# The sign of float64 weight words as an exponent bit, conversions queued behind a rectifier, and more unread products at a norm

## The chip, the cores and the metric

The kernel runs on one NeuronCore of a Trainium2 chip, in one launch. The metric is the device time of one execution in microseconds (us). TensorE does the matrix products, VectorE and ScalarE the elementwise work, GpSimd (POOL in the rows) some of it, and SyncE (SP) issues the transfers.

## The reference

A linear attention over 32 learned memories, then a Fourier mixing of tokens and features, a norm and a feed-forward layer with a residual. Eight batches of 576 tokens, 8 heads of 64 features, so 512 features; all float32.

```python
a = softmax(phi, over seq)                       # (b, h, s, 32)
k_m, v_m = a^T k, a^T v                          # (b, h, 32, 64)
x = softmax(q k_m^T / 8) v_m                     # heads joined: (8, 576, 512)
u = x + real(fft(fft(x, axis=1), axis=2))
un = (u - mean(u)) / sqrt(var(u) + 1e-6)
out = u + relu(un @ w_ch1) @ w_ch2               # w_ch1 512 x 2048, w_ch2 2048 x 512
```

The two weight matrices arrive as float64 words and are read as pairs of 32-bit words; the kernel itself makes float32 of them.

## The kernel before, in words

The 4608 tokens are 36 tiles of 128, taken two at a time as 18 *chunks*. The hidden width of 2048 is cut into 8 *units* (`NW`) of 256: unit j holds 1 MB of `w_ch1` and 1 MB of `w_ch2` as float64. A generator (`background`) makes the tiles of `u` batch by batch; the main loop advances it between units.

**Start.** Batch 0's attention is computed in float32, then its mixing, then `norm_chunk(0)` (called after `keep_busy(KEEP[4])`): bn_stats per tile (L777), a power on GpSimd (L787), the normalised tile `un` (L788), eight transposes on TensorE into `pt_unT` (L803), and copies on ScalarE (L804). `keep_busy(n)` (L262 to 266) issues 2n products of `identf` with itself into a PSUM tile `idle` that nothing reads.

**Chunk 0, the direct stage.** Chunk 0's feed-forward runs in float32 straight from the converted weights, unit by unit: `prepare_w1(j)` converts unit j of `w_ch1`, `ffn1_direct(j)` makes the hidden values (L821, two halves `ph`, 8 float32 products in the rows for each) and rectifies them on ScalarE (L824), `stage_w2(j)` converts unit j of `w_ch2`, `ffn2_direct(j)` accumulates the output `po` (L838, 8 in the rows for a unit). Beside it batch 1's scores run (`psc`, L576 to L613), and each unit is split into a float16 high and low part for the later chunks (`split_w1`, L953 to L958).

**The conversion** is `to_f32` (L907 on). `hi` is the upper 32-bit word of a float64 (sign, 11 exponent bits, 20 mantissa bits), `lo` the lower one. ScalarE reads `hi` as a float32 and writes its absolute value times 2^-112 (L919), which brings the exponent into 8 bits' room; VectorE shifts the word left by 3 (L921), ors in the sign bit taken from `hi` (L922), and ors in the top 3 bits of `lo` (L932). Then ScalarE squares the result and sums it (L943) for a scale; a one-column product `as_sq` (L239) adds over the partitions. Unit 0 of each matrix is converted in two halves (`HALVED`).

**Order.** All is written with a tile framework that sorts each engine's instructions by its own estimate. `issue_after(x)` makes instructions stand behind x in x's own engine queue; `after(names, ...)` does so for marked instructions, and the tables `GATE1` and `GATE2` name those that unit j's conversions stand behind. Each engine works its queue strictly in order.

**Later chunks** (1 to 17) use three float16 products for each float32 one: `ffn1` (L288, tile `ph`) and `ffn2` (L874).

Of the kernel before, what the change touches and what calls it, by code (L numbers as in the profile page):

```python
# [10 lines left out]
F32 = mybir.dt.float32  # L11
# [4 lines left out]
AF = mybir.ActivationFunctionType  # L16
ALU = mybir.AluOpType
# [22 lines left out]
NHS = 7  # L40
STEPS = 2
NX = 2
KEEP = [8, 18, 0, 0, 10, 4, 3]
GATE1 = [["et0"]] + [["un1", "uh0"]] * 7
GATE2 = [["at0"]] + [["un1", "uh0"]] * 7
NA = 2
# [87 lines left out]
def kernel(  # L134
# [10 lines left out]
    nc = tc.nc  # L145
# [116 lines left out]
    def keep_busy(n):  # L262

        with tc.issue_after(marks["pe"].ins) if "pe" in marks else nullcontext():
            for _ in range(2 * n):
                nc.tensor.matmul(idle, lhsT=unread[:, :P], rhs=unread, start=True, stop=True)
# [51 lines left out]
    def pooling_f32(b, pl, pf, rest):  # L318
# [11 lines left out]
        if b == 0:  # L330
            keep_busy(KEEP[1])
        for g in range(2):
# [7 lines left out]
        for g in range(2):  # L340
# [5 lines left out]
            if b == 0:  # L346
                keep_busy(KEEP[5 + g])
            marks[f"et{b}"] = nc.vector.tensor_copy(out=et32[:, g, :4], in_=pt.rearrange("p (t c) -> p t c", c=P))
# [270 lines left out]
    def pair_transpose(b, g, ahl, attnT):  # L619
        transpose(attnT[:, g], ahl.rearrange("p t c -> p (t c)"), b == 0, f"attnT_{b}_{g}")  # L620

    def values(b, vmf, ivs, ahl):
# [4 lines left out]
        if b < NX:  # L627
# [3 lines left out]
            if b == 0:  # L631
                marks["pe"] = marks["sum"]
                for g in range(3):
                    pair_transpose(b, g, ahl.pop(g), attnT)
                keep_busy(KEEP[2])
            norm_scale(sg, isg, top, 1, 14, f"v_{b}")
# [177 lines left out]
    def ffn1_direct(j):  # L814

        w = w1_f32(j).rearrange("p (k c) -> p k c", k=NK)
        h = h_f32(j)
        for f in range(UB):
            ph = ps1.tile([P, CH, P], F32, tag="h", name=f"ph_0_{j}_{f}", padded_shape=[P, 4, P])
            for k in range(NK):  # L820
                nc.tensor.matmul(  # L821
                    ph, lhsT=w[:, k, f * P : (f + 1) * P], rhs=unTs[0][:, k], start=(k == 0), stop=(k == NK - 1)
                )
            nc.scalar.activation(h[:, f], ph, AF.Relu)  # L824

    def h_slot(c, j):
        return hring[:, (4 + c * NW + j) % NW]
# [82 lines left out]
    def to_f32(stages, dst, key):  # L910

        if key in HALVED:
            stages = [s[:, i * UW : (i + 1) * UW] for s in stages for i in range(2)]
        n = UW // len(stages)
        for i, stage in enumerate(stages):
            wf = stage.rearrange("p (a b) -> p a b", b=2)
            hi, lo = wf[:, :, 1], wf[:, :, 0]
            part = dst[:, n * i : n * (i + 1)]
            nc.scalar.activation(part, hi.bitcast(F32), AF.Abs, scale=2.0**-112)  # L919
            d = part.bitcast(I32)  # L920
            nc.vector.tensor_scalar(out=d, in0=d, scalar1=3, scalar2=None, op0=ALU.logical_shift_left)  # L921
            marks[key] = nc.vector.scalar_tensor_tensor(  # L922
                out=d, in0=hi, scalar=-0x80000000, in1=d, op0=ALU.bitwise_and, op1=ALU.bitwise_or
            )
            lu = lo.bitcast(U32)
            if key in LP:
                marks[key] = nc.vector.tensor_scalar(
                    out=lu, in0=lu, scalar1=29, scalar2=None, op0=ALU.logical_shift_right
                )
                nc.gpsimd.tensor_tensor(out=d, in0=lo, in1=d, op=ALU.add)  # L930
            else:
                marks[key] = nc.vector.scalar_tensor_tensor(  # L932
                    out=part.bitcast(U32),
                    in0=lu,
                    scalar=29,
                    in1=part.bitcast(U32),
                    op0=ALU.logical_shift_right,
                    op1=ALU.bitwise_or,
                )
        sq = tiny("sq", 2, 4)  # L940
        dump = elt.rearrange("p l c -> p (l c)").bitcast(BF16)[:, :UW]
        with soon(int(key[2:])):
            marks["sq" + key] = nc.scalar.activation(dump, dst, AF.Square, accum_out=sq[:, 0:1])  # L943
            return all_sum(sq[:, 0:1], 1, f"sq_{key}")
# [55 lines left out]
    marks = {}  # L1000
# [77 lines left out]
    for g in range(NG):  # L1078
        with tc.issue_after(marks["q"].ins):
            marks["q"] = nc.sync.dma_start(  # L1080
                out=phi_next[:, :, g], in_=raw[1, g, :, KV:KVP].rearrange("p (t c) -> p t c", t=NST)
            )
    keep_busy(KEEP[0])
    first = [load_pair(0, 0)]
# [40 lines left out]
    def after(names, fn, *a):  # L1125
        with ExitStack() as st:
            for m in names:
                st.enter_context(tc.issue_after(marks[m].ins))
            return fn(*a)
# [17 lines left out]
    while made < 2:  # L1147
        made, room = next(bg)
    keep_busy(KEEP[4])
    unTs = {0: norm_chunk(0)}  # L1150
    hs = {c: [] for c in range(n_chunks)}
    po = [ps2.tile([P, 512], F32, tag="o", name=f"po_0_{t}") for t in range(CH)]
    for j in range(NW):
        if j > 2:
            load_weights(j)
        after(GATE1[j], prepare_w1, j)
        ffn1_direct(j)
        after(GATE2[j], stage_w2, j)
        ffn2_direct(j, po)
        with soon(j):  # L1160
            split_w1(j)
        advance(0, steps=STEPS)
        if made >= 2 * CH and 1 not in unTs:
            unTs[1] = norm_chunk(1)
# [20 lines left out]
    for n in range(NW, n_steps):  # L1185
        c, j = divmod(n, NW)
# [75 lines left out]
```

## Time and profile before

| | |
|---|---|
| Median of 3 runs | 950.43 us (950.41 to 950.98) |
| Profiled execution, its own time | 948.53 us |
| Its span | 946.8 us |
| TensorE busy | 930.0 us (98%), 7784 products |
| VectorE busy | 560.6 us (59%), 1291 instructions |
| ScalarE busy | 458.8 us (48%) |
| GpSimd busy | 219.2 us (23%) |

The span is what the profiler sees from the first to the last instruction; the execution's own time is 1.7 us longer, and the median 1.9 us above that. Busy shares are means over the whole kernel: the start, the direct stage and the later chunks have different limits, so the rows below are read stretch by stretch. A granted clock of 1.00 is TensorE's 2.4 GHz, 0.50 its 1.2 GHz.

### The profile page before, as it was taken

The page shows a single profiled execution, that of the slowest core. Times are in us where ns is not written, and L with a number is a line of the kernel's source. Part 1 is how long each engine was busy: PE and PEld are TensorE (multiplying, and loading weights), DVE is VectorE, ACT ScalarE, POOL GpSimd, SP SyncE. Part 2 cuts the span into 40 slices and gives each one's busy share as a digit, 9 for nine tenths or more (in the row PEclk, how much of TensorE's full clock was granted, in tenths as well). Part 3 has the DMA queues.
Part 4 walks back from the last instruction along what each step waited for, and adds up shares of the span by engine and source line. Part 5 has one row for each costly group of instructions (what it writes and reads, how often), then busy time and mean ns, then how long its engine had stood idle before and what let it go on. Part 6 is the DMA issues. An engine that isn't in the chain of part 4 may idle for free.

```text
span 946.8 us, 18932 instructions
## 1 busy us (share of the span) xinstructions
PE 930.0 (98%) x7784; PEld 662.8 (70%) x7784; DVE 560.6 (59%) x1291; ACT 458.8 (48%) x920; POOL 219.2 (23%) x255
## 2 busy tenths in 40 slices
PE   9989899999999999999999999999999999999998
PEld 8966568677777777777767777777776667666664
DVE  5989987767665666666424666667656675221111
ACT  4666757856465545654414554756446544211110
POOL 1302533414132222423200241223121331200000
PEclk9999899999999999999999999999999999999999
DMA  9947540454126242644102641263133201110000
GB/s 316 388 179 266 168 117 1 83 136 102 43 49 172 60 86 42 153 101 93 23 24 59 139 102 43 56 153 103 31 69 73 82 19 48 28 45 22 2 23 23
DMA packets 115959, 88.09 MB, mean 93 GB/s; under 512 B 100384, under 2 KB 100384, under 8 KB 113824
## 3 DMA queue, kind: packets, MB, share of 16 engines
q1 hardware_dynamic: 115872, 86.87, 34.5%
q8 instruction: 61, 1.00, 0.5%
q14 instruction: 26, 0.21, 0.1%
HBM read 58.15 MB, written 9.44 MB: 71 GB/s over the span
## 4 chain that ended last, share of the span: by engine, by line
PE 82%; DVE 7%; ACT 2%; issue 1%; POOL 1%; DMA 0%; DVEq 0%
PE ph L288 36%; PE po L874 36%; PE pm L288 2%; PE pp_t L288 2%; PE px_t L288 1%; PE psc L288 1%; PE pa L684 1%; DVE w2s L922 1%; DVE w1t L932 1%; DVE w2s L932 1%; PE pv L657 1%; PE pp_t L727 1%; DVE w1t L958 1%; DVE w1t L922 1%; PE pf L362 0%
## 5 line engine op out<-in xcount | busy, mean ns | idle before, releaser
L288 PE MATMUL ph<-unring,w1t 128*128 128x256 f16 x3264 | 389.0, 273 | 0.0
L874 PE MATMUL po<-w2s,hring 128*128 128x512 f16 x1632 | 378.8, 379 | 0.0
L288 PEld LDWEIGHTS <-w1t 128*128 128x128 f16 x3264 | 314.8, 98 | 64.0 <-issue 3.3
L874 PEld LDWEIGHTS <-hring 128*128 128x128 f16 x1632 | 157.1, 98 | 157.8 <-issue 0.4
L865 DVE SCALAR_TENSOR_TENSOR hring<-ph,hring 128x512 f16<-128x512 f32 x136 | 93.0, 684 | 155.2 <-ACT hring L864 155.1
L864 ACT ACTIVATE hring<-ph 128x512 f16<-128x512 f32 x136 | 80.3, 590 | 166.7 <-PE ph L288 163.8
L592 POOL TENSOR_TENSOR aring<-aring,scratch 128x384 f32<-128x384 f32 x28 | 24.2, 864 | 177.9 <-DVE scratch L590 169.0
L787 POOL TENSOR_TENSOR scratch<-scratch,small 128x1 f32<-128x1 f32 x36 | 22.6, 632 | 170.3 <-DVE scratch L786 118.5
L288 PEld LDWEIGHTS <-stg 128*128 128x128 f16 x1152 | 45.1, 98 | 8.5 <-issue 0.5
L808 POOL TENSOR_TENSOR ud<-un,ud 128x1024 f16<-128x1024 f32 x17 | 36.2, 2128 | 28.6 <-ACT ud L807 28.6
L586 ACT ACTIVATE aring<-aring,scratch 128x384 f32<-128x384 f32 x24 | 14.7, 611 | 54.6 <-DVE aring L585 54.6
L509 POOL TENSOR_TENSOR stg<-rawt,stg 128x640 f16<-128x640 f32 x12 | 17.4, 1454 | 87.3 <-ACT rawt L508 87.3
L838 PE MATMUL po<-w2s,hring 128*128 128x512 f32 x64 | 33.6, 657 | 3.4 <-DVE w2s L932 3.3
L611 ACT CAST aeo<-eo 128x384 f16<-128x384 f32 x30 | 15.3, 510 | 44.0 <-DVE eo L608 44.0
L886 DVE SCALAR_TENSOR_TENSOR uring<-po,small,uring 128x512 f32<-128x512 f32 x34 | 24.4, 742 | 16.9 <-PE po L874 16.9
L763 DVE SCALAR_TENSOR_TENSOR uring<-px_t,scratch,share 128x256 f32<-128x256 f32 (+1 forms) x80 | 34.1, 476 | 0.1
L749 DVE SCALAR_TENSOR_TENSOR share<-pp_t,scratch,small 128x257 f32<-128x257 f32 (+1 forms) x48 | 21.1, 481 | 21.1 <-ACT small L746 21.1
L602 POOL TENSOR_TENSOR aring<-aring 128x128 f32<-128x128 f32 x56 | 33.0, 609 | 2.0
L576 DVE TENSOR_REDUCE scratch<-psc 128x12 f32<-128x384 f32 x32 | 17.6, 551 | 26.4 <-PE pm L288 14.0
L288 PE MATMUL pm<-et,stg 128*128 128x64 f16 (+1 forms) x740 | 32.3, 195 | 0.3 <-DMA et<-elt 0.3
L613 DVE SCALAR_TENSOR_TENSOR aeo<-aeo,small,eo 128x128 f16<-128x128 f16 x30 | 24.1, 803 | 12.0 <-ACT aeo L611 12.0
L821 PE MATMUL ph<-unring,w1t 128*128 128x256 f32 x128 | 30.4, 384 | 0.7 <-DVE w1t L932 0.7
(271 smaller groups left out, 1227.8 us busy)
## 6 DMA issues: line engine op xcount, KB each, us to landing
out<-uring SPq DMA_DIRECT2D x36, 256.0 KB, 2.4
rawt<-in_raw SPq DMA_DIRECT2D x13, 640.0 KB, 4.6
stg<-in_raw SPq DMA_DIRECT2D x13, 640.0 KB, 5.1
stg<-in_w SPq DMA_DIRECT2D x7, 1024.0 KB, 5.0
rawt<-in_raw SPq DMA_DIRECT2D x15, 384.0 KB, 3.3
stg<-in_raw SPq DMA_DIRECT2D x15, 384.0 KB, 3.2
phs<-in_raw SPq DMA_DIRECT2D x28, 160.0 KB, 3.4
w2s<-in_w SPq DMA_DIRECT2D x4, 1024.0 KB, 10.2
```

The lines of the kernel that those rows point to most:

```text
L288: m = nc.tensor.matmul(out, lhsT=lhsT, rhs=rhs, start=start, stop=stop)
L592: eng.tensor_tensor(out=a, in0=a, in1=sm.unsqueeze(2).to_broadcast([P, 12, M]), op=ALU.mult)
L602: eng.tensor_tensor(out=a2[:, i : i + 4], in0=a[:, 0:4], in1=a[:, 4:8], op=op)
L613: marks[f"s{b}_{g}"] = nc.vector.scalar_tensor_tensor(out=lo[:, :4], in0=hi[:, :4], scalar=mk[:, 64:65], in1=eov[:, :4], op0=ALU.mult, op1 ...
L763: nc.vector.scalar_tensor_tensor(out=u[rows, hs], in0=px[rows, hs], scalar=igx[rows], in1=tm[rows, w * NJ + half : w * NJ + half + 256], o ...
L808: marks[f"ul{c}"] = nc.gpsimd.tensor_tensor(out=ud[:, 1], in0=un, in1=ud[:, 0], op=ALU.subtract)
L821: nc.tensor.matmul(ph, lhsT=w[:, k, f * P : (f + 1) * P], rhs=unTs[0][:, k], start=(k == 0), stop=(k == NK - 1))
L838: nc.tensor.matmul(po[t], lhsT=h[:, f, t], rhs=w[:, f], start=(j == 0 and f == 0), stop=(j == NW - 1 and f == UB - 1),)
L864: nc.scalar.activation(h[:, 0], phv, AF.Relu)
L865: nc.vector.scalar_tensor_tensor(out=h[:, 1], in0=phv, scalar=0.0, in1=h[:, 0], op0=ALU.max, op1=ALU.subtract)
L874: nc.tensor.matmul(po[t], lhsT=hs[j][:, lh, f * 2 + t], rhs=w2s[:, j * UB + f, lw, :], start=(j == 0 and f == 0 and i == 0), stop=(j == NW ...
L886: nc.vector.scalar_tensor_tensor(out=u, in0=po[t], scalar=cout if c else 0.5, in1=u, op0=ALU.mult, op1=ALU.add)
```

## The change

Three edits. (1) ScalarE's absolute value becomes its parametric rectifier (Prelu): out = x for x above 0, alpha times x below, with alpha = -2^32, behind the same scale. A negative weight comes out positive with its exponent 32 higher, which is bit 28 of the word; the shift by 3 moves bit 28 into the sign's place. The instruction that or-ed the sign in (L922 before) is gone: 20 of them. (2) The second rectifier of unit j's hidden values is marked `h{j}`, and from unit 2 on the conversions of unit j stand behind `h{j-2}` in ScalarE's queue. (3) `KEEP[4]` goes from 10 to 28: 56 unread products in place of 20 ahead of chunk 0's transposes.

```diff
-KEEP = [8, 18, 0, 0, 10, 4, 3]
+KEEP = [8, 18, 0, 0, 28, 4, 3]
...
-            nc.scalar.activation(h[:, f], ph, AF.Relu)
+            marks[f"h{j}"] = nc.scalar.activation(h[:, f], ph, AF.Relu)
...
-            nc.scalar.activation(part, hi.bitcast(F32), AF.Abs, scale=2.0**-112)
+
+            nc.scalar.activation(part, hi.bitcast(F32), AF.Prelu, scale=2.0**-112, alpha=-(2.0**32))
             d = part.bitcast(I32)
             nc.vector.tensor_scalar(out=d, in0=d, scalar1=3, scalar2=None, op0=ALU.logical_shift_left)
-            marks[key] = nc.vector.scalar_tensor_tensor(
-                out=d, in0=hi, scalar=-0x80000000, in1=d, op0=ALU.bitwise_and, op1=ALU.bitwise_or
-            )
...
-        after(GATE1[j], prepare_w1, j)
+        after(GATE1[j] + ([f"h{j - 2}"] if j >= 2 else []), prepare_w1, j)
         ffn1_direct(j)
-        after(GATE2[j], stage_w2, j)
+        after(GATE2[j] + ([f"h{j - 2}"] if j >= 2 else []), stage_w2, j)
```

In the changed kernel the conversion on ScalarE is L920, the shift L922, the or of the low bits L930, the square L941, the split's first part L951. The framework sorts the queues anew, so the order moves in many places; three matter.

VectorE just ahead of chunk 0's norm, where `w2s` is unit 0 of `w_ch2` in two halves, `share` and `uring` the mixing of the first two tiles; before the change:

```order
L921 TENSOR_SCALAR w2s<-w2s 128x512 x2
L922 SCALAR_TENSOR_TENSOR w2s<-w2s 128x512 x2
L932 SCALAR_TENSOR_TENSOR w2s<-w2s 128x512
L749 SCALAR_TENSOR_TENSOR share<-pp_t_617,scratch,small 128x257 x2
L932 SCALAR_TENSOR_TENSOR w2s<-w2s 128x512
L763 SCALAR_TENSOR_TENSOR uring<-px_t_633,scratch,share 128x256 x2
L763 SCALAR_TENSOR_TENSOR uring<-px_t_644,scratch,share 128x256 x2
```

The same place of VectorE's queue in the changed kernel:

```order
L922 TENSOR_SCALAR w2s<-w2s 128x512 x2
L930 SCALAR_TENSOR_TENSOR w2s<-w2s 128x512 x2
L749 SCALAR_TENSOR_TENSOR share<-pp_t_617,scratch,small 128x257 x2
L763 SCALAR_TENSOR_TENSOR uring<-px_t_633,scratch,share 128x256 x2
L763 SCALAR_TENSOR_TENSOR uring<-px_t_644,scratch,share 128x256 x2
```

The two sign instructions are gone and both low-bit instructions now stand ahead of the mixing.

ScalarE from the copies of chunk 0's transposed tile (L804) to unit 0's rectifiers (L824), before the change:

```order
L804 COPY unring<-pt_unT_691 128x4x128
L919 ACTIVATE w1t<-w1t 128x1024
L919 ACTIVATE w2s<-w2s 128x1024
L919 ACTIVATE w1t<-stg 128x1024
L919 ACTIVATE w2s<-stg 128x1024
L953 ACTIVATE w1t<-w1t,small 128x1024
L746 ACTIVATE small<-pp_t_745,scratch 128x255
L824 ACTIVATE hring<-ph_0_0_713 128x256
L943 ACTIVATE elt,scratch<-w1t 128x1024
L824 ACTIVATE hring<-ph_0_1_719 128x256
```

The same stretch of ScalarE's queue in the changed kernel:

```order
L804 COPY unring<-pt_unT_727 128x4x128
L920 ACTIVATE w1t<-w1t 128x1024
L920 ACTIVATE w2s<-w2s 128x1024
L951 ACTIVATE w1t<-w1t,small 128x1024
L746 ACTIVATE small<-pp_t_777,scratch 128x255
L941 ACTIVATE elt,scratch<-w1t 128x1024
L824 ACTIVATE hring<-ph_0_0_747 128x256
L824 ACTIVATE hring<-ph_0_1_753 128x256
L920 ACTIVATE w1t<-stg 128x1024
L920 ACTIVATE w2s<-stg 128x1024
```

The two conversions out of `stg`, those of unit 2, stood ahead of unit 0's rectifiers and now stand behind the second of them.

ScalarE in the middle of the direct stage, from unit 3's second rectifier to unit 4's second, in the changed kernel (`ahring`, `aeo`, `aring` belong to batch 1's scores):

```order
L824 ACTIVATE hring<-ph_3_1_975 128x256
L920 ACTIVATE w1t<-stg 128x1024
L920 ACTIVATE w2s<-hring 128x512
L920 ACTIVATE w2s<-uring 128x512
L611 CAST aeo<-eo 128x12x32
L586 ACTIVATE aring<-aring 128x384
L824 ACTIVATE hring<-ph_4_0_1035 128x256
L941 ACTIVATE elt,scratch<-w1t 128x1024
L941 ACTIVATE elt,scratch<-w2s 128x1024
L951 ACTIVATE w1t<-w1t,small 128x1024
L824 ACTIVATE hring<-ph_4_1_1041 128x256
```

Unit 5's conversions stand right behind unit 3's rectifier, and their squares stand ahead of unit 4's second one.

## Rows read from the trace of the kernel before

**Rows 1.** Busy time by stretch: us, then busy (instructions) of each engine, clock, DMA.

```profile
core 0: us, PE busy (x) PEld busy (x) DVE busy (x) ACT busy (x) POOL busy (x), PEclk, DMA share, GB/s
20.00:30.00 10.00, 10.00 (x92) 10.00 (x91) 9.97 (x28) 4.67 (x12) 1.56 (x2) 1.00 1.03 415
...
57.80:128.00 70.20, 64.58 (x277) 42.66 (x274) 70.03 (x131) 50.60 (x86) 20.04 (x18) 0.95 0.56 187
128.00:940.00 812.00, 811.67 (x7028) 572.46 (x7029) 446.83 (x1034) 377.97 (x766) 184.64 (x206) 1.00 0.29 69
```

**Rows 2.** TensorE in order of time around the norm: start, length, engine, line, names, count.

```profile
44.86 1.48 PE L288 MATMUL pp_t<-vh,at 128*128 128x257 f16 x12
...
47.07 2.35 PE L266 MATMUL idle<-identf 128*128 128x256 f16 x20
53.69 1.94 PE L803 MATMUL pt_unT<-identf,un 128*128 128x128 f32 x8 [4.27 <-DVE un L788]
...
55.52 1.91 PE L288 MATMUL pp_t<-vh,at 128*128 128x257 f16 x12
...
57.83 3.67 PE L821 MATMUL ph<-unring,w1t 128*128 128x256 f32 x16
```

**Rows 3.** Busy time by stretch, columns as in rows 1, around the transposes.

```profile
53.00:54.00 1.00, 0.31 (x2) 0.34 (x3) 0.93 (x2) 0.00 (x0) 0.58 (x1) 0.52 0.06 26
...
56.00:57.00 1.00, 1.00 (x9) 0.81 (x8) 0.31 (x4) 1.00 (x2) 0.00 (x0) 0.78 0.07 16
```

**Rows 4.** VectorE in order of time ahead of the norm.

```profile
45.95 1.30 DVE L922 SCALAR_TENSOR_TENSOR w2s<-w2s 128x512 int32<-128x512 int32 x2
47.15 0.70 DVE L932 SCALAR_TENSOR_TENSOR w2s<-w2s 128x512 uint32<-128x512 uint32 x1
...
53.00 1.16 DVE L788 TENSOR_SCALAR un<-uring,scratch 128x512 f32<-128x512 f32 x2 [0.60 <-POOL scratch L787]
```

**Rows 5.** TensorE in order of time in the direct stage.

```profile
77.77 1.96 PE L838 MATMUL po<-w2s,hring 128*128 128x512 f32 x4
...
81.40 1.45 PE L288 MATMUL psc<-scratch,rawt 128*128 128x64 f32 x12
...
94.78 3.69 PE L821 MATMUL ph<-unring,w1t 128*128 128x256 f32 x16
101.80 8.31 PE L838 MATMUL po<-w2s,hring 128*128 128x512 f32 x12 [3.32 <-DVE w2s L932]
...
121.97 1.13 PE L821 MATMUL ph<-unring,w1t 128*128 128x256 f32 x4 [0.72 <-DVE w1t L932]
...
127.99 0.40 PE L657 MATMUL pv<-hring,share 64*32 64x512 f16 x4 [1.45 <-ACT share L644]
```

**Rows 6.** VectorE by line, 57.8 to 128 us: busy, mean ns, idle before.

```profile
L958 DVE SCALAR_TENSOR_TENSOR w1t<-w1t,small 128x1024 f16<-128x1024 f32 x4 | 6.8, 1710 | 0.0
...
L921 DVE TENSOR_SCALAR w1t<-w1t 128x1024 int32<-128x1024 int32 (+1 forms) x8 | 5.2, 651 | 1.0 <-ACT w1t L919 1.0
L922 DVE SCALAR_TENSOR_TENSOR w1t<-stg,w1t 128x1024 int32<-128x1024 int32 x4 | 4.9, 1213 | 0.0
...
L922 DVE SCALAR_TENSOR_TENSOR w2s<-hring,w2s 128x512 int32<-128x512 int32 x1 | 2.6, 2611 | 0.0
...
L932 DVE SCALAR_TENSOR_TENSOR w1t<-w1t 128x1024 uint32<-128x1024 uint32 x2 | 2.4, 1204 | 0.0
```

**Rows 7.** ScalarE by line, 57.8 to 128 us.

```profile
L943 ACT ACTIVATE elt<-w1t 128x1024 bf16<-128x1024 f32 x7 | 7.4, 1056 | 1.9 <-DVE w1t L932 1.7 <-DVE small L260 0.2
...
L953 ACT ACTIVATE w1t<-w1t,small 128x1024 f16<-128x1024 f32 x6 | 6.9, 1145 | 1.4 <-DVE w1t L958 1.4
L824 ACT ACTIVATE hring<-ph 128x256 f32<-128x256 f32 x15 | 5.7, 380 | 2.7 <-PE as_sq L239 1.8 <-PE ph L821 0.9
L919 ACT ACTIVATE w1t<-stg 128x1024 f32<-128x1024 f32 x4 | 4.6, 1158 | 1.6 <-DMA stg<-in_w 1.6
```

**Rows 8.** ScalarE's only table load, in order of time.

```profile
0.73 1.28 ACT L185 ACT_TABLE_LOAD   x1 [0.73 <-PEq L1250]
```

## The prediction

> **What bounds the kernel now.** Read the stretches first. From 128 to 940 us TensorE is busy for 811.67 of 812.00 us at a granted clock of 1.00 [rows 1]: nothing that frees VectorE or ScalarE there can show. The direct stage, 57.8 to 128 us, is another matter: there VectorE is busy 70.03 of 70.20 us, TensorE 64.58, ScalarE 50.60, and the clock is 0.95 [rows 1]. VectorE is the full engine, and TensorE is what pays. TensorE's own list in order of time then shows where. Up to 98 us its products stand back to back; after that come three holes, 3.32 us, 0.72 us and 1.45 us long, the first two ended by VectorE's last conversion step and the third by a ScalarE copy [rows 5]. Behind the first hole 12 products of `po` take 8.31 us, where 4 of them took 1.96 us at 77.77 us [rows 5]; three times 1.96 is 5.9, so 2.4 us more go there to a lower clock. The stage thus loses 3.32 + 0.72 + 1.45 + 2.4 = 7.9 us of TensorE, and could not be shorter than 70.2 - 7.9 = 62.3 us.
>
> A second loss lies just ahead, at chunk 0's norm. TensorE issues its 20 unread products at 47.07 us, then stands idle for 4.27 us until VectorE has written `un` [rows 2]. The granted clock is 0.52 in the microsecond in which it starts again and has come back in part, to 0.78, by 56 to 57 us [rows 3]. So the transposes and the mixing product behind them run slowly: 12 `pp_t` products take 1.91 us at 55.52 and took 1.48 us at 44.86 [rows 2].
>
> **The change part by part.** *The sign off VectorE.* Twenty L922 instructions go: two halves of unit 0 of each matrix ahead of the norm, and the fourteen conversions of units 1 to 7 in the direct stage (two of these in halves). In the stage one of 1024 words takes 1.21 us [rows 6], 1.13 from start to start, so 14 x 1.13 = 15.8 us; one half took 2.61 us, 1.9 above its like [rows 6], and goes too. VectorE's work there falls from 70.0 to 52.3 us, under TensorE's 62.3. TensorE's three holes and the slow stretch behind the first then have no cause left in VectorE's throughput, and up to 7.9 us come back. ScalarE's 50.6 us stay as they are if Prelu costs what the absolute value did.
>
> *Prelu's price.* The trace has no Prelu. Three other functions over 1024 words cost 1.06 (square), 1.15 (scaled copy) and 1.16 us (absolute value) [rows 7]; I take 1.16, the row with the same operands. If it made two passes it would be 2.3 us: 14 x 1.16 = 16.2 us more on ScalarE, 66.8 in all, 4.5 above TensorE's floor. A gain is bounded by the square: 14 x 0.1 = 1.4 us off an engine that isn't full, so nothing.
>
> *The conversions behind the rectifiers.* No instruction is added; ScalarE's order changes. Unit j+2's two conversions now follow the second rectifier of unit j, and unit j is two units ahead of their use, so a conversion has about one unit of TensorE's time to get through ScalarE and VectorE: 62.3 / 8 = 7.8 us on average, against 1.16 for the conversion, 0.65 for the shift and 1.2 for the or [rows 6, 7], 3.0 us in all for the first matrix and about 5 for the second. What is queued behind the conversions is the next thing to be late. By the changed order a turn of ScalarE from one unit's second rectifier to the next one's holds two conversions (2.3), two squares (2.1), a split (1.15) and two rectifiers (0.76) [rows 7], and some 1.4 us of the scores' steps: 7.7 us of its own. The squares wait for VectorE, which I put at 1.5 us a turn. That makes 9.2 us in the units with scores, where TensorE needs 3.69 + 2 x 1.96 + 1.45 [rows 5], less some 0.6 of overlap, so 8.5; without scores 7.7 against 7.1. Over six turns ScalarE falls behind by 4 x 0.7 + 2 x 0.6 = 4.0 us, and TensorE gives 3.6 us of grace, since a second half's rectified values are read only after one half of `po` and the next `ph`. Little is left, some 0.4 us; to it I add about 2 us for single instructions that stretch, as the 2.61 did. So 2.5 us of new waits, with 0 and 6 as ends: 7.9 - 2.5 = **5.4 us gained** in the stage.
>
> *Norm and unread products.* Ahead of the norm VectorE loses two sign instructions at 45.95 us, 1.2 us from start to start, directly on its queue to `un` [rows 4]. Two more go at about 20 us, where VectorE is busy 9.97 of 10 us [rows 1]; how much of those 1.2 us arrives is unknown, between all and nothing. `un` is then ready 1.2 to 2.4 us sooner, which would start the transposes at 52.5 to 51.3. But 56 products at 2.35 / 20 us each [rows 2] take 6.6 us: begun at 47.07, or up to 1.2 us earlier, they end at 53.7 to 52.5. The products become the last wait, by a little. I take a start 0.8 us earlier, ends 0 and 1.2. With no hole ahead of them the transposes run at the full clock: 8 in 1.94 us at half clock [rows 2, 3], so about half of that saved, and 0.43 on the mixing product, 1.4 together; I take 1.3, and as ends 0.5 (a hole remains) and 1.8. Sum: **2.1 us gained**, 0.5 to 3.0.
>
> *Afterwards.* Chunks 1 to 17 need the splits of both matrices, made by ScalarE, VectorE and GpSimd while TensorE runs the first of them. All of this moves forward with the stage, and the changed order places `w_ch2`'s first splits only after two of chunk 1's hidden units rather than six. The 0.33 us of idle time there [rows 1] can grow; I take 0.3 more, ends 0 and 1.5.
>
> Sum: 2.1 + 5.4 - 0.3 = 7.2 us. The profiled execution's own 948.53 becomes 941.3; the median stands 1.9 above it, so **943.2 us**.
>
> **Rivals.** *ScalarE's queue takes VectorE's place (slower).* If nearly all of VectorE's work in a turn lies between a conversion and the second square, a turn is 1.16 + 6.9 + 1.06 + 1.15 + 0.38 = 10.7 us, with 6.9 from two shifts and two ors (3.7), a split (1.2) and the scores' reads (some 2). The loss is then 6 x (10.7 - 8.0) - 3.6 = 12.6 us in place of 7.9, and with the norm's 2.1 the time is 953.0. The point is a turn of about 10.6 us, where the loss reaches 7.9 + 2.1 + 1.9. With a split at the mean of 1.71 [rows 6] and one stretched row a turn it is 13 us and the time near 965. For it: the squares do stand ahead of the next rectifier, and rows of VectorE stretch. Against: VectorE has 10 us of slack in the stage, and a split can wait behind the squares' inputs. Chance 0.10. Between the two, with turns of 10.0 to 10.6 us, lies no change: 0.07.
>
> *Prelu sits in another table (slower).* ScalarE's only table load takes 1.28 us [rows 8]. If every group of conversions switched there and back, eight groups of units 2 to 7 would add 16 x 1.28 = 20.5 us, so ScalarE would need 71.1 us of the stage against 70.2 now, and the three groups before add 7.7 more ahead of the stage: some 955 us with the norm's gain. The changed kernel's ScalarE queue holds one table load, as before, at L185, which speaks against it: 0.02. The Trainium skill (ScalarE: Activation LUTs, What ACT_TABLE_LOAD costs) puts a switch at about 2.66 us with the drain around it. By that the stage would need 50.6 + 16 x 2.66 = 93 us, and the time would be near 977. No row here shows a drain, as there is no second load.
>
> *Weight loads come late (less gained).* ScalarE waited 1.6 us for loads into `stg` [rows 7]; those buffers are refilled every second unit, only after VectorE has read them, and a stage of 65 us gives each less time. If such waits reach TensorE at two or three places, 2 to 4 us of the 5.4 are lost: 945 to 947. Chance 0.21. That the clock still falls at the norm would cost 1.3: 944.5, inside the forecast.
>
> **How the numbers follow.** A measurement of this kernel can tell about 0.2%, 1.9 us, from no change. Forecast with waits up to 4 us: 0.60. Late loads: 0.21. These two make faster, 0.81. No change 0.07. Slower 0.12. The lowest of the sums is 950.43 - 3.0 - 7.9 = 939.5; the highest of the faster cases with its bounds is 950.43 - 0.5 - 1.9 + 1.0 = 949.0. 939.5 to 949.0 leaves out the slower cases and part of no change, 0.15 to 0.2.
>
> **What would show it.** Right: VectorE no longer full in the direct stage, some 53 of 65 us; TensorE's holes there below 3 us in sum and the clock at 1.00 all through; the transposes in about 1 us, straight behind the unread products; Prelu near 1.16 us. Wrong: `ph` or `po` waiting for `hring` out of L824, or L824 standing behind a square that waits for VectorE (the first rival); ScalarE's conversion waiting for transfers (the third); a second table load; or new holes after the stage, ended by the splits of `w_ch2`.

## The result, and the profile after

The changed kernel takes **943.17 us** (median of 4 runs, 941.25 to 943.25) against 950.7 us for the kernel before in the same comparison (4 runs, 950.41 to 951.17): a ratio of 0.9915, 95% interval 0.9898 to 0.9933. The forecast was 943.2.

That the median agrees to the tenth owes something to luck. The prediction's sum was made against a profiled execution (948.53) that stood 1.9 us below its median. The profiled execution of the changed kernel, 943.25, is no lower than its median. From profile to profile the gain is 5.3 us, where the sum said 7.2; the spans go from 946.8 to 941.4. The two profiles are not alike, though. Three of the changed kernel's four executions took 943.1 to 943.3 us at a mean granted clock of 0.996, and one took 941.25 at 1.000, which by my estimate (0.0005 x 940 us x 2) leaves room for less than 1 us at half clock. The kernel before stood at 950.4 to 951.2 in this comparison, and at 948.0 to 949.0 in about half of its executions in the later ones. So the profile of before is of one of its shorter executions and the profile of the changed kernel of one of its longer ones. Short against short the gain is 7.3 us (948.53 to 941.25), median against median 7.5. No trace shows the execution of 941.25. In the comparisons further down some executions, of the kernel before too, took some 18 us longer at a mean clock of 0.97 to 0.98: the ratios leave them out, the medians count them.

The page of the changed kernel, its first part:

```profile
PE 931.6 (99%) x7820; PEld 666.2 (71%) x7820; DVE 548.0 (58%) x1271; ACT 459.6 (49%) x920; POOL 217.5 (23%) x255
```

VectorE has its 20 instructions and 12.6 us less. Next the busy time by stretch, columns as in [rows 1]:

```profile
57.80:128.00 70.20, 65.92 (x308) 43.51 (x307) 59.28 (x131) 52.96 (x93) 26.39 (x29) 0.95 0.65 208
...
110.00:120.00 10.00, 10.00 (x33) 5.74 (x34) 8.52 (x21) 8.44 (x16) 3.86 (x7) 0.70 0.30 89
```

VectorE is no longer full in the direct stage: 59.28 of 70.20 us, where it was 70.03 [rows 1]. Yet TensorE is busy for only 1.3 us more of the same stretch, and its clock there is 0.95 as before, with 0.70 in one piece of 10 us. So the bound is gone and the loss is not.

TensorE in order of time around the norm, after:

```profile
46.13 6.28 PE L266 MATMUL idle<-identf 128*128 128x256 f16 x56
52.25 0.93 PE L803 MATMUL pt_unT<-identf,un 128*128 128x128 f32 x7
...
53.21 1.48 PE L288 MATMUL pp_t<-vh,at 128*128 128x257 f16 x12
...
55.14 3.67 PE L821 MATMUL ph<-unring,w1t 128*128 128x256 f32 x16
```

Here all went as meant. The hole of 4.27 us [rows 2] is gone, the transposes stand directly behind the 56 unread products, and `pp_t` takes 1.48 us in place of 1.91. Chunk 0's first `ph` starts at 55.14 us in place of 57.83: **2.7 us gained**, 0.94 of it because the unread products already begin at 46.13 in place of 47.07 (how much of that is the change's is said further down).

TensorE in order of time in the middle of the direct stage, after:

```profile
102.43 1.98 PE L838 MATMUL po<-w2s,hring 128*128 128x512 f32 x4 [0.46 <-ACT hring L824]
104.25 1.89 PE L821 MATMUL ph<-unring,w1t 128*128 128x256 f32 x8
109.83 3.78 PE L838 MATMUL po<-w2s,hring 128*128 128x512 f32 x4 [3.69 <-ACT hring L824]
113.40 3.14 PE L821 MATMUL ph<-unring,w1t 128*128 128x256 f32 x8
```

The holes ended by VectorE's conversion [rows 5] are gone, and a new one of 3.69 us stands in their place, ended by ScalarE's rectifier L824. Behind it `po` takes 3.78 us (1.98 at 102.43) and `ph` 3.14 (1.89 at 104.25), at the lower clock (0.50 from 110 to 114 us): 3.05 us more. With the 0.46 the stage loses **7.2 us**, where it lost 7.9. ScalarE's queue shows why. ScalarE in order of time over the same stretch, after:

```profile
101.99 0.38 ACT L824 ACTIVATE hring<-ph 128x256 f32<-128x256 f32 x1
102.27 1.05 ACT L941 ACTIVATE elt<-w1t 128x1024 bf16<-128x1024 f32 x1
...
105.05 0.74 ACT L492 ACTIVATE stg<-rawt 128x640 bf16<-128x640 f32 x1 [1.64 <-DVE small L257]
...
105.79 0.72 ACT L492 ACTIVATE stg<-rawt 128x640 bf16<-128x640 f32 x1
...
106.51 0.83 ACT L495 ACTIVATE stg<-rawt 128x768 bf16<-128x768 f32 x1
...
107.33 1.04 ACT L941 ACTIVATE elt<-w2s 128x1024 bf16<-128x1024 f32 x1
...
108.37 1.13 ACT L951 ACTIVATE w1t<-w1t,small 128x1024 f16<-128x1024 f32 x1
109.41 0.36 ACT L824 ACTIVATE hring<-ph 128x256 f32<-128x256 f32 x1
```

Between unit 5's first rectifier (101.99) and its second (109.41) stand two squares of unit 6, a split, and three rows that belong to batch 2: L492 and L495 square its keys, values and queries for a scale, and put the unread squares into `stg`. From 105.05 to 107.33 they take 2.28 us, and they come after 1.64 us of idle time. The profile names a short VectorE step (L257) as the releaser, but the row just before it is the one that fits: VectorE's low-bit step of unit 6 reads `stg`, and ends at 104.96. VectorE in order of time, after:

```profile
99.59 1.70 DVE L930 SCALAR_TENSOR_TENSOR w1t<-stg,w1t 128x1024 uint32<-128x1024 uint32 x1
...
101.95 3.01 DVE L930 SCALAR_TENSOR_TENSOR w2s<-stg,w2s 128x1024 uint32<-128x1024 uint32 x1
```

And GpSimd over the same time:

```profile
99.26 0.95 POOL L600 TENSOR_TENSOR ahring<-aring,ahring 128x320 f16<-128x320 f32 x1 [1.61 <-ACT ahring L599]
101.36 2.52 POOL L954 TENSOR_TENSOR w1t<-w1t 128x1024 f16<-128x1024 f32 x1 [1.15 <-ACT w1t L953]
103.84 1.65 POOL L612 TENSOR_TENSOR aeo<-eo,aeo 128x256 f16<-128x256 f32 x1
```

A low-bit step alone takes 1.21 us (1.20 in [rows 6]). Here one takes 3.01 and one 1.70, and each ends 1.08 us after the GpSimd row that was running when it began (101.36 + 2.52 = 103.88, to 104.96; 99.26 + 0.95 = 100.21, to 101.29). The 2.61 us of [rows 6] has the same shape. The Trainium skill (SBUF — State Buffer, SBUF: two separate sides) says that VectorE and GpSimd share one pair of ports to that memory as an exclusive lock: a VectorE step with two inputs there and a GpSimd step block each other for the whole instruction. By that rule the step runs only when GpSimd's has ended; the rows agree, GpSimd's L612 among them: it began while the low-bit step ran and took 1.65 us, where it takes 0.67 elsewhere.

### The profile page after: what moved, and what is told of

It is laid out like the page before. It is cut to its first block, busy times and chain, and to the rows that moved or that the text cites. A ratio compares the mean times of both kernels' runs of the same rounds, so it can differ in the third digit from the quotient of the medians.

```text
span 941.4 us, 18994 instructions
## 1 busy us (share of the span) xinstructions
PE 931.6 (99%) x7820; PEld 666.2 (71%) x7820; DVE 548.0 (58%) x1271; ACT 459.6 (49%) x920; POOL 217.5 (23%) x255
## 4 chain that ended last, share of the span: by engine, by line
PE 88%; DVE 3%; ACT 1%; issue 1%; POOL 0%; DVEq 0%; ACTq 0%
PE ph L288 38%; PE po L874 37%; PE pm L288 2%; PE pp_t L288 2%; PE px_t L288 2%; PE psc L288 1%; PE po L838 1%; PE pa L684 1%; DVE w2s L930 1%; PE ph L821 1%; PE pv L657 1%; PE pp_t L727 1%; PE pf L362 1%; DVE w1t L930 0%; ACT elt L941 0%
## 5 line engine op out<-in xcount | busy, mean ns | idle before, releaser
L509 POOL TENSOR_TENSOR stg<-rawt,stg 128x640 f16<-128x640 f32 x12 | 17.7, 1475 | 90.2 <-ACT rawt L508 90.2
L763 DVE SCALAR_TENSOR_TENSOR uring<-px_t,scratch,share 128x256 f32<-128x256 f32 (+1 forms) x80 | 33.9, 475 | 0.2 <-PE px_t L288 0.2
L604 DVE TENSOR_TENSOR eo<-aring 128x128 f32<-128x128 f32 x29 | 29.5, 1018 | 5.9 <-POOL aring L602 5.9
## 6 DMA issues: line engine op xcount, KB each, us to landing
w2s<-in_w SPq DMA_DIRECT2D x4, 1024.0 KB, 10.8
```

What stands on the lines that cost most here:

```text
L604: nc.vector.tensor_tensor(out=eo[:, 1:3, 0], in0=ap[:, 1:3, 0], in1=ap[:, 1:3, 1], op=ALU.add)
L763: nc.vector.scalar_tensor_tensor(out=u[rows, hs], in0=px[rows, hs], scalar=igx[rows], in1=tm[rows, w * NJ + half : w * NJ + half + 256], o ...
```

## The experiments

Times are medians; a ratio is to the kernel before run beside it, with its 95% interval. 0.001 of a ratio is 0.95 us. The kernel before itself lay between 948.0 and 951.6 us in the different comparisons, so ratios are compared first; a difference of 0.001 between two comparisons can still be the kernel before's. In the kernels with moved rows ScalarE's and TensorE's lines behind the edit are one higher (L825 is the rectifier, L839 `po`).

### Each edit alone on the kernel before

Only the unread products:

```diff
-KEEP = [8, 18, 0, 0, 10, 4, 3]
+KEEP = [8, 18, 0, 0, 28, 4, 3]
```

> The kernel before with the 56 unread products alone; VectorE keeps its sign instructions and the conversions their old places. Theory (each edit pays where it stands, the stage's loss is VectorE's): VectorE writes un as late as before, at about 53.7 us of the span; the products end at 47.07 + 6.28 = 53.35, so the 4.27 us hole shrinks under 0.5 us and the clock stays at 1.00 through the transposes, which is worth 1.3 to 1.4 us. VectorE stays full in the direct stage, 99% or more, and the stage keeps its loss of 8 us. Time 949.0 to 949.6. Rival (a head start at the norm is lost again, since VectorE sets the end of the stage): within 0.3 us of the kernel before.

948.94 us, ratio 0.9984 (0.9970 to 0.9998). TensorE in order of time at the norm:

```profile
53.79 1.19 PE L803 MATMUL pt_unT<-identf,un 128*128 128x128 f32 x8 [0.34 <-DVE un L788]
```

The hole falls from 4.27 to 0.34 us and the transposes from 1.94 to 1.19. First `ph` starts at 57.07, 0.76 us earlier. VectorE stays full (62.00 of the 62 us from 58 to 120 us).

Only the sign:

```diff
-            nc.scalar.activation(part, hi.bitcast(F32), AF.Abs, scale=2.0**-112)
+            nc.scalar.activation(part, hi.bitcast(F32), AF.Prelu, scale=2.0**-112, alpha=-(2.0**32))
...
-            marks[key] = nc.vector.scalar_tensor_tensor(
-                out=d, in0=hi, scalar=-0x80000000, in1=d, op0=ALU.bitwise_and, op1=ALU.bitwise_or
-            )
```

> The kernel before with the Prelu edit alone: 20 sign instructions fewer, 20 unread products, conversions free to run ahead. Theory (VectorE was the full engine): un is ready about 2 us sooner, at some 51.6; the hole at the norm stays, about 3 us, and with it the lower clock in the transposes; in the direct stage VectorE is under 90% busy and the stage's loss falls from 8 to 2 or 3 us, so 942.5 to 945. Rival (ScalarE's queue takes VectorE's place, which the third edit is there to prevent): rectifiers stand behind conversions and squares, TensorE waits for hring, the loss stays at 6 us or more, 947 to 949.5.

947.16 us, ratio 0.9967 (0.9952 to 0.9982). VectorE falls to 55.86 of 62 us from 58 to 120 us, as in the changed kernel (55.81), yet only 3.1 us come back. TensorE in order of time, three of its holes:

```profile
52.43 1.18 PE L803 MATMUL pt_unT<-identf,un 128*128 128x128 f32 x8 [3.27 <-DVE un L788]
...
97.58 1.88 PE L288 MATMUL psc<-scratch,stg 128*128 128x64 f32 x12 [1.61 <-DMA stg<-in_raw]
...
113.30 1.98 PE L838 MATMUL po<-w2s,hring 128*128 128x512 f32 x4 [1.15 <-ACT hring L824]
```

Without the other edits the hole at the norm stays, and in the stage TensorE already waits for ScalarE, but longer for a transfer: 1.61 us at 97.58, behind which four products of `po` take 3.29 us. At 180.90 us it waits 2.62 us more for another transfer (`et<-elt`). So the time lies in the rival's range, though only 1.15 us of the stage's holes is ScalarE's. What made these transfers late was not looked at.

Only the gate, the conversions behind the rectifier:

```diff
-            nc.scalar.activation(h[:, f], ph, AF.Relu)
+            marks[f"h{j}"] = nc.scalar.activation(h[:, f], ph, AF.Relu)
...
-        after(GATE1[j], prepare_w1, j)
+        after(GATE1[j] + ([f"h{j - 2}"] if j >= 2 else []), prepare_w1, j)
...
-        after(GATE2[j], stage_w2, j)
+        after(GATE2[j] + ([f"h{j - 2}"] if j >= 2 else []), stage_w2, j)
```

> The kernel before with the conversions of unit j behind the second rectifier of unit j - 2, alone. Theory (VectorE full): VectorE has as much to do as before and now starts on units 2 to 7 later, so the stage's loss stays or grows: 950 to 953, VectorE at 97% or more of the stage. Rival (the order was the trouble, not VectorE's work): TensorE's holes shrink to under 4 us and the time falls to 946 to 948.

950.95 us, ratio 1.0017 (1.0004 to 1.0030): no gain, rather a loss. VectorE is still nearly full (60.57 of 62 us), and a rectifier is late all the same. TensorE in order of time:

```profile
120.99 6.68 PE L838 MATMUL po<-w2s,hring 128*128 128x512 f32 x8 [3.16 <-ACT hring L824]
```

The three alone make 0.0016 + 0.0033 - 0.0017 = 0.0032, 3.0 us; together they make 0.0085, 8.1 us. Each edit makes the framework sort the queues anew, so none of these is a pure price. The next two runs ask the same from the other side.

### One edit undone in the changed kernel

The gate undone:

```diff
-        after(GATE1[j] + ([f"h{j - 2}"] if j >= 2 else []), prepare_w1, j)
+        after(GATE1[j], prepare_w1, j)
...
-        after(GATE2[j] + ([f"h{j - 2}"] if j >= 2 else []), stage_w2, j)
+        after(GATE2[j], stage_w2, j)
```

> The changed kernel with the second edit alone undone: unit j's conversions are no longer held behind h{j-2}. Theory A (the gate is needed once the other two edits are in: it keeps the rectifiers ahead of the two stg conversions of the next units): new holes in front of po or ph, ended by ScalarE's rectifier L824, and a time of 945 to 947, about what the two other edits gave alone (1.6 + 3.4 us below 950.5). Theory B (the gate alone was worth nothing, +0.4 us, and the holes come from the squares): 942.5 to 944, as the changed kernel.

944.31 us, ratio 0.9939 (0.9924 to 0.9954): between the two theories, and its interval meets that of the changed kernel. It decides nothing by itself; the last run of the next section does.

The unread products back at 20:

```diff
-KEEP = [8, 18, 0, 0, 28, 4, 3]
+KEEP = [8, 18, 0, 0, 10, 4, 3]
```

> The changed kernel with KEEP[4] back at 10, 20 unread products in place of 56. If the unread products earn their part by the clock: a hole of about 3 us, ended by VectorE's un at L788, stands ahead of the transposes; they start some 0.6 us earlier but run at a granted clock near 0.5, so that chunk 0's first ph starts 0.5 to 1.3 us later than in the changed kernel (56.5 against 55.14 with the hole of the run with the sign alone); time 943.7 to 944.5. Rival: since un is ready at 51.6, an idle TensorE there costs nothing and the earlier start pays for the clock: 942.8 to 943.3, and ph_0_0 at 55.1 or before.

945.32 us, ratio 0.9947 (0.9932 to 0.9962): 0.0032 or 3.0 us by the ratios, and 2.2 by the medians, more than expected. TensorE in order of time at the norm:

```profile
51.97 1.94 PE L803 MATMUL pt_unT<-identf,un 128*128 128x128 f32 x8 [3.26 <-DVE un L788]
...
53.80 2.73 PE L288 MATMUL pp_t<-vh,at 128*128 128x257 f16 x12
...
57.39 3.98 PE L821 MATMUL ph<-unring,w1t 128*128 128x256 f32 x16
```

The hole has the length expected, and the transposes do start 0.28 us sooner than in the changed kernel. But the granted clock stays at 0.50 from 52 to 58 us here, `pp_t` takes 2.73 us in place of 1.48, and the first `ph` starts 2.25 us later. So the unread products pay by the clock, as predicted, and in this execution by more than I had put. How long the low clock lasts differs: in the kernel before, behind a hole of 4.27 us, it was back at 1.00 by 57 us, some 3 us after TensorE's start; here it is back at 58 us, 6 us after.

### The rows of batch 2 moved away

The test of the reading above: in the changed kernel, L492 and L495 of batch 2 (their first group alone) stand behind unit 7's second rectifier.

```diff
-        for w in range(2):
-            nc.scalar.activation(
-                kvs[0][:, :, w, :].bitcast(BF16), kv[:, :, w, :], AF.Square, accum_out=am[:, 1 + w : 2 + w]
-            )
-        nc.scalar.activation(
-            kvs[1][:, 0:3].rearrange("p t w c -> p (t w c)").bitcast(BF16), q, AF.Square, accum_out=am[:, 0:1]
-        )
+        with tc.issue_after(marks["h7"].ins) if b == 2 and g == 0 else nullcontext():
+            for w in range(2):
+                nc.scalar.activation(
+                    kvs[0][:, :, w, :].bitcast(BF16), kv[:, :, w, :], AF.Square, accum_out=am[:, 1 + w : 2 + w]
+                )
+            nc.scalar.activation(
+                kvs[1][:, 0:3].rearrange("p t w c -> p (t w c)").bitcast(BF16), q, AF.Square, accum_out=am[:, 0:1]
+            )
```

> The changed kernel with one more order: batch 2's three squares of k, v and q (ScalarE, 2.3 us in its trace at 105.05 to 107.33 us) stand behind unit 7's second rectifier. Theory (ScalarE's queue is the new bound, at one turn): in the changed kernel unit 5's second rectifier stood behind these three and behind the square of unit 6's second matrix, and TensorE waited 3.69 us for it and then ran 6.6 us at a low clock. Without the three the rectifier comes 2.3 us sooner, the hole shrinks to about 1.4 us and, if the clock then holds, 3 us more come back: 938 to 941. Rival (the hole is VectorE's, whose last conversion step took 3.01 us there, and it moves to the next wait): 942.5 to 943.5 with a hole of 3 us or more, ended by VectorE.

**939.93 us** (939.79 to 940.86), ratio 0.9896 (0.9879 to 0.9912): its times lie below all of the changed kernel's, though the intervals of the ratios overlap. TensorE in order of time:

```profile
107.68 1.98 PE L839 MATMUL po<-w2s,hring 128*128 128x512 f32 x4 [1.44 <-ACT hring L825]
109.50 1.89 PE L822 MATMUL ph<-unring,w1t 128*128 128x256 f32 x8
```

ScalarE in order of time:

```profile
105.17 1.06 ACT L942 ACTIVATE elt<-w2s 128x1024 bf16<-128x1024 f32 x1 [1.66 <-DVE small L257]
...
107.26 0.36 ACT L825 ACTIVATE hring<-ph 128x256 f32<-128x256 f32 x1
```

The hole shrinks by 2.25 us, close to the 2.28 us of the moved rows, and the clock no longer falls: `po` and `ph` behind the hole take 1.98 and 1.89 us. ScalarE's idle 1.66 us ahead of unit 6's square stays, since the low-bit step takes 3.01 us here too. From span to span (941.4 to 938.0) 3.4 us arrive of the 5.0 that the stage's rows show (2.25 + 0.22 + 3.05, less a new hole of 0.52). Of the other 1.6, 0.77 is a hole at 177.07 us, ended by a transfer (`et<-elt`), that the changed kernel's trace doesn't have.

The same move in the kernel before the change (with the mark `h{j}` that it needs):

> The kernel before with nothing but batch 2's squares moved behind the last unit's second rectifier. If these squares are a fault of the queue that the kernel before has in equal measure: 946 to 948 (some 3 us gained, as in the changed kernel). Rival, which I hold likelier: before the change VectorE is full in the stage and ends the holes itself with its last conversion step, so the squares cost nothing there: 949 to 951, and the holes stay ended by L932.

948.47 us, ratio 0.9996 (0.9987 to 1.0005): nothing. TensorE in order of time:

```profile
101.48 8.34 PE L839 MATMUL po<-w2s,hring 128*128 128x512 f32 x12 [3.31 <-DVE w2s L933]
```

There VectorE ends the large hole, and is busy 61.86 of 62 us. So there the rows of batch 2 cost TensorE nothing. Two things differ from the changed kernel, and this run does not part them: VectorE ends the holes, and the rows stand elsewhere, at 115.66 to 117.93 us ahead of unit 6's first rectifier, where the hole in front of `po` is 0.1 us.

The move with the gate undone:

> The changed kernel with batch 2's squares behind h7 and without the gate on the conversions (second edit undone). If the gate's worth in the changed kernel (1.1 us between the two medians of the run without it and the changed kernel) was only that it pushed back those squares: 939 to 940.5, as with the gate. Rival (the conversions ahead of the rectifiers cost TensorE by themselves): 941 to 943, with holes ahead of po ended by L825 behind two conversions.

943.05 us, ratio 0.9941 (0.9928 to 0.9953), against 0.9896 with the gate: 0.0045, or 4.3 us (3.1 by the medians), with intervals apart. TensorE in order of time:

```profile
61.17 1.98 PE L839 MATMUL po<-w2s,hring 128*128 128x512 f32 x4 [1.15 <-ACT hring L825]
...
107.33 1.98 PE L839 MATMUL po<-w2s,hring 128*128 128x512 f32 x4 [0.90 <-ACT hring L825]
111.49 0.63 PE L658 MATMUL pv<-hring,share 64*32 64x512 f16 x8 [2.17 <-ACT share L645]
...
113.91 3.78 PE L822 MATMUL ph<-unring,w1t 128*128 128x256 f32 x8
```

ScalarE in order of time, unit 0's rectifiers:

```profile
60.76 0.63 ACT L825 ACTIVATE hring<-ph 128x256 f32<-128x256 f32 x2
```

The gate is a gain where VectorE is not full, and a small loss alone. One part of what it cures is plain: here unit 2's two conversions out of `stg` (56.20 and 57.25 us, 2.3 us together) stand ahead of unit 0's rectifiers, and TensorE waits 1.15 us for these. Beyond that the scores' steps and `share` (L645) come late too; which of the conversions does that harm was not taken apart. Nor does the move gain anything without the gate: 0.9939 with the gate undone, 0.9941 with the move as well.

### What is left of the hole

Each unit's own squares held behind the unit before's second rectifier, on top of the move:

```diff
-        with soon(int(key[2:])):
-            marks["sq" + key] = nc.scalar.activation(dump, dst, AF.Square, accum_out=sq[:, 0:1])
+        j = int(key[2:])
+        with soon(j):
+            with tc.issue_after(marks[f"h{j - 1}"].ins) if j >= 2 else nullcontext():
+                marks["sq" + key] = nc.scalar.activation(dump, dst, AF.Square, accum_out=sq[:, 0:1])
```

> The kernel with batch 2's squares moved behind h7, and besides each unit's own squares (unit 2 on) held behind h{j-1}, so that both rectifiers of a unit stand ahead of the squares. If what is left of the stage's loss (1.44 us ahead of po, ended by L825) is ScalarE's queue with squares ahead of a rectifier: that hole falls under 0.5 and the time is 938.5 to 939.5. Rival: the squares then crowd behind the rectifier, the conversions of the next unit come later, and a hole appears ahead of ph or po that VectorE's low-bit step or the split ends: 940 to 942.

939.96 us, ratio 0.9898 (0.9882 to 0.9914): no change from the move alone. TensorE in order of time, its only holes between 46 and 128 us:

```profile
109.42 0.41 PE L658 MATMUL pv<-hring,share 64*32 64x512 f16 x8 [1.04 <-ACT share L645]
...
118.47 0.30 PE L677 MATMUL pa<-ct,aeo 128*128 128x290 f16 x1 [1.52 <-DVE aeo L614]
```

No rectifier is late any more, and as the rival had it other steps are. The trace is that of the shortest of the four executions, 938.06 us at a mean clock of 1.000; the other three took 939.9 to 940.4 at 0.998, and what they lost besides is not shown.

Unit 4's split off GpSimd, on top of the move:

```diff
-        if j in L2:
+        if j in L2 and j != 4:
             nc.scalar.activation(src, src, AF.Copy, scale=s)
             nc.gpsimd.tensor_tensor(out=w[:, 1], in0=src, in1=w[:, 0], op=ALU.subtract)
         else:
             nc.vector.scalar_tensor_tensor(
...
```

> The kernel with batch 2's squares moved behind h7, and unit 4's split of w_ch1 taken off GpSimd (2.52 us there at 101.4): its low part is made by VectorE (one more 1.3 us row there) in place of a ScalarE copy and GpSimd's subtraction. If GpSimd's row is what held VectorE's low-bit step of unit 6 for 3.01 us (it ended 1.1 us after GpSimd's row did, the length that such a step has alone): that step takes 1.2 to 1.3 us, unit 6's square starts 1 to 2 us earlier, the hole of 1.44 us goes, and the time is 938.5 to 939.6. Rival (the stretch is the low-bit step's own, or from ScalarE or a transfer): it stays near 3 us, VectorE is 1.3 us fuller, and the time is 940 to 941.5.

939.19 us, ratio 0.9888 (0.9874 to 0.9901). VectorE in order of time:

```profile
99.03 1.28 DVE L923 TENSOR_SCALAR w1t<-w1t 128x1024 int32<-128x1024 int32 x1
...
100.90 1.66 DVE L931 SCALAR_TENSOR_TENSOR w1t<-stg,w1t 128x1024 uint32<-128x1024 uint32 x1
...
103.01 1.21 DVE L931 SCALAR_TENSOR_TENSOR w2s<-stg,w2s 128x1024 uint32<-128x1024 uint32 x1
```

GpSimd in order of time:

```profile
98.94 0.82 POOL L601 TENSOR_TENSOR ahring<-aring,ahring 128x320 f16<-128x320 f32 x1 [1.63 <-ACT ahring L600]
100.81 0.67 POOL L613 TENSOR_TENSOR aeo<-eo,aeo 128x256 f16<-128x256 f32 x1 [1.05 <-ACT aeo L612]
```

The disputed step takes 1.21 us in place of 3.01: it was GpSimd's row that held it. But the hole did not go as I had expected: it is 1.65 us here, with a second of 0.52. Unit 6's first square now waits, because its shift (1.28) and its low-bit step (1.66) began beside GpSimd's next two rows and again end behind them, by 0.55 and 1.08 us.

All three such splits on VectorE, on top of the move:

```diff
-        if j in L2:
+        if False:
```

> The kernel with batch 2's squares moved behind h7, and all three of GpSimd's splits of w_ch1 (units 2, 4 and 6) made by VectorE in place of a ScalarE copy and GpSimd's subtraction. ScalarE loses 3 x 1.13 us, GpSimd 7.1 us, VectorE gains 3 x 1.3 us less what stood behind GpSimd's rows (1.8 us with unit 4's). If VectorE rows standing behind GpSimd's were a good part of what makes ScalarE's squares late: 938.3 to 939.2, at or under the 939.2 of the run with unit 4's alone. Rival (those rows only moved the wait elsewhere; the squares ahead of the rectifier stay): 939.2 to 940.5, with holes ended by L825 of the same size.

**937.79 us**, ratio 0.9879 (0.9864 to 0.9894), the lowest of all and clear of the changed kernel's interval. TensorE's only holes in the stage:

```profile
106.09 1.98 PE L839 MATMUL po<-w2s,hring 128*128 128x512 f32 x4 [0.57 <-ACT hring L825]
...
110.70 1.98 PE L839 MATMUL po<-w2s,hring 128*128 128x512 f32 x4 [0.89 <-ACT hring L825]
```

VectorE took on three rows of 1.3 us and is busy 55.96 of the 62 us from 58 to 120, as with the move alone (55.97): what it gained from rows no longer behind GpSimd's paid for them. But the edit also takes three copies of 1.14 us out of ScalarE's queue, the one that makes the rectifiers late, and this run does not part that from what VectorE gained.

Both small edits, the unit's squares behind the rectifier and unit 4's split on VectorE:

> Batch 2's squares behind h7, each unit's own squares behind the earlier unit's second rectifier, and unit 4's split on VectorE. If the two small edits act on different holes (L825 ahead of po; VectorE's low-bit step): 937.5 to 939, the fastest. Rival: each only turns the wait over to another instruction (share at L645, aeo at L614, a transfer into stg): 939 to 940.5, not told from either alone.

937.90 us, ratio 0.9890 (0.9877 to 0.9903). The median lies in the range of the first theory, but the kernel before was lower too in that comparison (948.8); by the ratios this isn't told from either edit alone, as the rival had it. Its one hole in the stage, 1.14 us at 118.08, is again ended by L825. Nor are the five versions with moved rows and the gate told from one another by their times; what tells them apart is their holes.

## Why the prediction was right, and where not

**The norm and the unread products** (2.1 us, 0.5 to 3.0): right. 2.7 us came, with the products the last wait by a little, as the sum had it. The start 0.8 us earlier was 0.94, in part by luck: 0.43 of it lies between 30 and 40 us, where TensorE idles 0.4 to 0.7 us in every run with the sign instructions and not at all in those without; the rest lies in the first 20 us, where its idle time differs from run to run (1.6 to 2.7 us in all of them). The clock kept its full level. Putting the products back cost 2.25 us at that place.

**Prelu's price** (1.16 us): right. ScalarE by line in the direct stage, after:

```profile
L920 ACT ACTIVATE w1t<-stg 128x1024 f32<-128x1024 f32 x4 | 4.6, 1157 | 0.0
L920 ACT ACTIVATE w2s<-stg 128x1024 f32<-128x1024 f32 x3 | 3.5, 1153 | 0.0
```

Neither the two passes nor the rival of the other table came; there is one table load. The idle column also shows the third rival absent: these conversions did not wait for transfers.

**The direct stage** (5.4 us gained): this step failed in size. That VectorE would cease to be the bound was right, though its busy time in the window fell by 10.8 us (70.03 to 59.28) where the sum took off 17.7. The term mis-sized is the one for new waits, "2.5 us of new waits, with 0 and 6 as ends". The holes were 4.15 us; with the 3.05 us of lower clock behind the second, which the forecast did not price for new holes, 7.2 were lost. The holes came from ScalarE's turn, put at 9.2 us. The second rectifiers of units 1 to 4, after:

```profile
67.78 0.36 ACT L824 ACTIVATE hring<-ph 128x256 f32<-128x256 f32 x1
...
78.08 0.36 ACT L824 ACTIVATE hring<-ph 128x256 f32<-128x256 f32 x1
...
87.17 0.38 ACT L824 ACTIVATE hring<-ph 128x256 f32<-128x256 f32 x1
...
97.44 0.36 ACT L824 ACTIVATE hring<-ph 128x256 f32<-128x256 f32 x1
```

With unit 5's at 109.41 these are turns of 10.3, 9.1, 10.3 and 12.0 us, 10.4 in the mean. The squares' wait for VectorE is in them with 2.06, 0, 2.14 and 1.64 us, 1.5 in the mean, as put. Too small was "7.7 us of its own", counted from one printed piece of the order, unit 3's rectifier to unit 4's. That piece has no L953, ScalarE's copy ahead of a GpSimd split, which takes 1.14 us in every second turn (at 81.88 and 100.14 us), and none of batch 2's three rows, 2.28 us in unit 5's turn; moving these shortened the hole by 2.25. TensorE's own turns, from the end of one unit's last `ph` to the next one's, took 33.9 us for the four (67.71 to 101.57). So ScalarE fell 7.8 us behind. TensorE idled 4.15 of them, and the rest, some 3.6, is the grace that the forecast had put.

**The first rival** is what happened, in mechanism: a rectifier behind squares that wait for VectorE. Its turn of 10.7 us was near the measured 10.4. Its price of 12.6 us supposed six such turns against 8.0 us of TensorE's; there were four (units 6 and 7 took 7.2 and 8.7) against 8.5.

**Afterwards** (0.3 us lost): not told apart. From profile to profile 5.4 us of span came, 2.7 of them ahead of chunk 0's first `ph`; the other 2.7 lie in the stage and behind it, where the visible losses went from 7.9 to 7.2 only. (The 7.9 is 0.3 too low: from the start of the 12 products to the next row 8.14 us pass, and four take 1.80 from start to start at 77.77, so the lower clock took 2.7 and not 2.4.) TensorE's idle time from 128 to 200 us fell from 0.33 us to nothing, so the new holes that I feared there did not come in this run; in several of the others a hole of 0.4 to 2.6 us, ended by a transfer, stands there. Where the other 1.4 us came from is open: the interleaving of chunk 0 and chunk 1 is different, and no two stretches hold the same work.

**The sum**: 7.2 us was 5.3 from profile to profile, and 7.3 between the shorter executions of both kernels. The profiled execution of the changed kernel has the 3.05 us of lower clock; the one of 941.25 us, with a mean clock of 1.000, has no room for it. The median was met because the two profiled executions stand differently to their medians, because the norm gave 0.6 us more than its term, and because of 1.4 us whose place is open.

## What to carry to other kernels

When an engine that was full is relieved, its waits pass to the next queue that is strictly in order. Go through that queue for every turn, not for one typical turn, and count the rows of neighbouring work (here the next batch) that the sorter has put ahead of the instruction that TensorE waits for. A small edit there is worth nothing while the old bound stands (0.0004 in the kernel before), 2 to 3 us once it is gone (1.8 by the ratios, 3.2 by the medians), and again nothing without the gate (0.0002); and an edit that looks useless alone, as the gate, can be worth 3 to 4 us beside the others, so undo edits from the whole as well as trying them singly.

## What the runs showed of the hardware

That a VectorE step can take 3.01 us in place of 1.21 because of GpSimd was not in my sum, which put such stretches at "about 2 us" without a cause. Its length could have been read off the trace of before: the 2.61 us row of [rows 6] began beside a GpSimd split of 2.16 us. Taking GpSimd's three splits away brought the mean of the low-bit steps out of `stg` into `w2s` from 1.82 to 1.21 us. VectorE by line, 57.8 to 128 us, with the move alone:

```profile
L931 DVE SCALAR_TENSOR_TENSOR w2s<-stg,w2s 128x1024 uint32<-128x1024 uint32 x3 | 5.5, 1821 | 0.0
```

The same group with all three splits on VectorE:

```profile
L931 DVE SCALAR_TENSOR_TENSOR w2s<-stg,w2s 128x1024 uint32<-128x1024 uint32 x3 | 3.6, 1207 | 0.0
```

And TensorE's clock made a hole of 3.69 us cost 6.7 in the profiled execution of the changed kernel, while one of 1.44 us cost only itself in that of the kernel with the move.
